# A Fourier filter ahead of a SiLU feed-forward block: sums and differences first, second products in eighths of the TensorE array, the complex filter on VectorE

## The chip, the cores and the metric

The kernel runs on one core of one Trainium2 chip. The metric is the time of one execution on the device in microseconds (us); lower is better. A figure from "the trace" comes from the hardware profiler's record of one execution. For the kernel before, the profiler took an execution of its own (3203.65 us). All runs told here are in the same, fast, state.

## The reference, cut to what matters

```python
# x: (8, 3008, 256)   filt_r, filt_i: (1505, 256)   w_in: (256, 2048)   w_out: (2048, 256)
X = np.fft.rfft(x, axis=1)
Y = X * (filt_r + 1j * filt_i)[None, :, :]
y = np.fft.irfft(Y, n=3008, axis=1)              # (8, 3008, 256), then (24064, 256)
h = y @ w_in
g = h * (1.0 / (1.0 + np.exp(-h)))               # SiLU
out = g @ w_out
```

The two dense products do most of the arithmetic. The transforms are done as matrix products too, by factors of 3008 = 47 x 64.

## The kernel before: the parts that matter

The names of the products are the names in the profile. For each of the 8 batches:

- **pa**: first products of the forward transform (47 points), already packed as four tiles of 47 rows by 64 columns.
- **pb**: second products (64 points), each a full 128 x 128 matrix. VectorE multiplies the result by the real and by the imaginary part of the filter (two tiles `p`).
- **pc**: first products of the inverse. The complex filter is completed here, by adding two products with two tables (`e_t[:, 0]` and `e_t[:, 1]`) in PSUM.
- **pd**: last products of the inverse; they give `y`.
- **ph** and **po**: the two dense products, with SiLU on ScalarE in between.

The dense work of a batch is 96 units; a unit is one ph piece and one po piece. The transforms of batch b+1 are cut into pieces that are placed by hand between the units of batch b. Batch 0 has nothing to hide behind: its transforms, the loading of all tables, and the rounding of the weights (VectorE turns 64-bit weights into 32-bit, 16 times) make the opening. In what follows, the opening ends at the first ph.

```python
def load_filters(g):                       # 4 calls, 16 loads of 192 KB, all issued by ScalarE's queue
    gs = slice(6 * g, 6 * g + 6)
    for k, filt in enumerate((filt_r, filt_i)):
        for q in range(2):
            off, step = (6 * g * C, C) if q == 0 else ((N1 - 6 * g) * C, -C)
            nc.scalar.dma_start(out=f_t[k][32 * q:32 * q + 32, gs, :],
                in_=bass.AP(tensor=filt.tensor, offset=filt.offset + off,
                            ap=[[N1 * C, 32], [step, 6], [1, C]]))   # 32 partitions x 6 rows

def evac(dst, src):                        # PSUM is emptied by VectorE and ScalarE in turn
    flip[0] ^= 1
    if flip[0]:
        nc.vector.tensor_copy(out=dst, in_=src)
    else:
        nc.scalar.copy(out=dst, in_=src)

def stage1(u):                             # pa, 8 pieces per batch
    ...
    for i in range(2):
        for h in range(2):
            rows = slice(64 * h, 64 * h + N1)
            nc.tensor.matmul(out=ps[h][64 * i:64 * i + 64], lhsT=wf_t[rows, :],
                             rhs=xt[rows, 2 * i:2 * i + 2, :], start=True, stop=True)
    for h in range(2):
        evac(t1[:, h], ps[h])
    ...                                    # t1 to DRAM, later read back as t2

def stage2(u):                             # pb and pc, 12 + 12 pieces per batch
    ...
        for i in range(2):
            nc.tensor.matmul(out=ps[:, i, :], lhsT=d_t[:, 2 * u + i, :], rhs=t2[:, i, :],
                             start=True, stop=True)
        ...
        for k in range(2):
            nc.vector.tensor_tensor(out=pt, in0=ps, in1=f_t[k][:, 2 * u:2 * u + 2, :], op=ALU.mult)
    ...
        for i in range(2):
            for k in range(2):
                nc.tensor.matmul(out=ps[:, i, :], lhsT=e_t[:, k, 2 * w + i, :],
                                 rhs=pr[k][:, i, :], start=(k == 0), stop=(k == 1))
    ...

at = UNITS * b                             # UNITS is 96
pieces  = [(at - 94 + 2 * u, lambda u=u: stage1(u)) for u in range(8)]
pieces += [(at - 75 + 2 * u, lambda u=u: stage2(u)) for u in range(13)]
pieces += [(at - 44 + 5 * u, lambda u=u: stage3(u)) for u in range(8)]         # pd, first half of y
pieces += [(at + 4 + 5 * u, lambda u=u: stage3(8 + u)) for u in range(8)]      # pd, second half
...
pending += [(-90 + 3 * j, NJ, lambda j=j: round_weights(j)) for j in range(NJ)]  # NJ is 16
```

## Time and profile before

| | before |
|---|---|
| time, median of 3 (range) | 3205.25 us (3203.8 to 3206.78) |
| ScalarE's first evacuation of PSUM | at 27.0 us |
| last evacuation of stage 1 of batch 0 | at 55.3 us |
| first ph (end of the opening) | at 155.6 us |
| one steady batch (first pa to first pa, mean of six) | 385.5 us |

Read it as a sum: 155.6 us of opening, then eight batches of dense work in which TensorE has hardly a hole (busy 383.29 of 385 us in a steady batch, 929 to 1314 us). A change is worth what it takes off the opening plus what it takes off each of the seven batches in which a following batch's transforms run. The busy table, the chain and the piece lines are shown and read in the prediction.

### The profile page before, as it was taken

What the parts mean: (1) busy time and instruction counts of PE and PEld (TensorE: products, weight loads), DVE (VectorE), ACT (ScalarE), POOL (GpSimd) and SP (SyncE); (2) the same over time, 40 slices, a digit from 0 to 9 for tenths busy, and PEclk for the clock granted to TensorE, in tenths of its full rate; (3) what the DMA queues carried; (4) which work ended last, traced back from release to release, by engine and by line L of the source; (5) the groups of instructions that cost most, each with busy time, mean ns of one, the idle gap of its engine ahead of it and who ended that gap; (6) DMA issues with size and microseconds to landing.
All of it is one profiled execution on the core that took longest, in us unless ns stands there. A gap on an engine that the chain in (4) does not pass through costs nothing.

```text
span 3201.7 us, 29583 instructions
## 1 busy us (share of the span) xinstructions
PE 3105.9 (97%) x11928; PEld 2096.2 (65%) x11928; DVE 353.7 (11%) x629; ACT 584.1 (18%) x1048; POOL 466.2 (15%) x884
## 2 busy tenths in 40 slices
PE   4699999999999999999999999999999999999999
PEld 2457666676666766667665676657766576666666
DVE  5701000110001100011000110011100110000000
ACT  1021111211111111211112111121111211111111
POOL 2121101211012101111102120031101211010101
PEclk9799999999999999999999999999999999999999
DMA  7532111221112211222102220032101221000000
GB/s 216 141 95 62 35 31 38 85 57 31 28 46 82 53 28 33 60 71 51 33 22 80 63 53 20 22 96 63 40 17 42 84 64 35 17 18 17 13 7 13
DMA packets 92583, 165.17 MB, mean 52 GB/s; under 512 B 24560, under 2 KB 56416, under 8 KB 92320
## 3 DMA queue, kind: packets, MB, share of 16 engines
q1 hardware_dynamic: 51456, 83.40, 9.3%
q0 software_dynamic: 38400, 75.04, 8.9%
q10 hardware_dynamic: 2592, 4.85, 0.6%
q8 instruction: 94, 1.54, 0.2%
q14 instruction: 41, 0.34, 0.0%
HBM read 88.21 MB, written 74.97 MB: 51 GB/s over the span
## 4 chain that ended last, share of the span: by engine, by line
PE 94%; DMA 1%; issue 1%; ACT 0%; DVE 0%; POOL 0%; POOLq 0%; DVEq 0%; ACTq 0%; SPq 0%
PE po L283 41%; PE ph L269 40%; PE pc L223 5%; PE pd L246 4%; PE pb L205 2%; PE pa L183 2%; DMA out_dram<-o 1%; ACT t L149 0%; DMA t<-d 0%; POOL out_dram L296 0%; ACT g L272 0%; DVE o L147 0%; DVE p L214 0%; DMA d<-q 0%; ACT o L149 0%
## 5 line engine op out<-in xcount | busy, mean ns | idle before, releaser
L283 PEld LDWEIGHTS po<-w,g 128*128 128x128 f32 (+1 forms) x6144 | 1152.4, 188 | 493.0 <-issue 353.8
L283 PE MATMUL po<-w,g 128*128 128x256 f32 (+1 forms) x6144 | 1455.0, 379 | 7.7 <-DVE o L147 5.4
L269 PE MATMUL ph<-y,w 128*128 128x512 f32 (+1 forms) x3072 | 1429.1, 588 | 0.0
L269 PEld LDWEIGHTS ph<-y,w 128*128 128x128 f32 x3072 | 572.4, 191 | 426.8 <-issue 389.4
L272 ACT ACTIVATE g<-ph 128x512 f32<-128x512 f32 (+1 forms) x768 | 452.0, 589 | 1961.1 <-PE ph L269 1960.9
L296 POOL DMA_DIRECT2D out_dram<-o x432 | 223.5, 525 | 1544.2 <-DVE o L147 1081.5
L229 POOL DMA_DIRECT2D d<-q x192 | 114.0, 598 | 803.1 <-DVE q L147 480.6
L223 PE MATMUL pc<-p,e_t 128*128 128x256 f32 x768 | 187.5, 388 | 9.5 <-DVE p L214 9.5
L214 DVE TENSOR_TENSOR p<-pb,filt 128x512 f32<-128x512 f32 x192 | 123.5, 686 | 614.2 <-PE pb L205 614.1
L190 POOL DMA_DIRECT2D d<-t x256 | 128.5, 509 | 384.2 <-DVE t L147 220.5
L147 DVE COPY o<-po 128x256 f32<-128x256 f32 x96 | 40.8, 425 | 1228.2 <-PE po L283 1181.3
L223 PEld LDWEIGHTS pc<-p,e_t 128*128 128x128 f32 x768 | 149.0, 195 | 32.9 <-DVE p L214 9.4
L246 PEld LDWEIGHTS pd<-wi_t,t 96*128 96x128 f32 x1024 | 138.0, 200 | 40.0 <-ACT t L149 22.9
L246 PE MATMUL pd<-wi_t,t 96*128 96x94 f32 x1024 | 139.3, 282 | 20.2 <-ACT t L149 10.5
L205 PE MATMUL pb<-t,d_t 128*128 128x256 f32 x384 | 102.6, 391 | 21.2 <-issue 10.3
L183 PE MATMUL pa<-x,wf_t 47*64 47x512 f32 x512 | 84.7, 673 | 29.4 <-DMA x<-in_x_dram 17.6
L205 PEld LDWEIGHTS pb<-t,d_t 128*128 128x128 f32 x384 | 74.1, 195 | 36.8 <-issue 12.4
L147 DVE COPY y<-pd 128x376 f32<-128x376 f32 x64 | 35.2, 550 | 556.7 <-PE pd L246 556.7
L147 DVE COPY t<-pa 128x512 f32<-128x512 f32 x64 | 44.2, 691 | 416.1 <-PE pa L183 413.7
L149 ACT COPY q<-pc 128x512 f32<-128x512 f32 x48 | 28.1, 586 | 220.1 <-PE pc L223 220.1
L149 ACT COPY t<-pa 128x512 f32<-128x512 f32 x64 | 37.5, 586 | 130.9 <-PE pa L183 121.7
L149 ACT COPY y<-pd 128x376 f32<-128x376 f32 x64 | 30.2, 472 | 164.6 <-PE pd L246 164.6
(24 smaller groups left out, 179.1 us busy)
## 6 DMA issues: line engine op xcount, KB each, us to landing
d<-t POOLq DMA_DIRECT2D x256, 96.0 KB, 2.8
t<-d SPq DMA_DIRECT2D x192, 128.0 KB, 2.7
d<-q POOLq DMA_DIRECT2D x192, 128.0 KB, 2.6
t<-d SPq DMA_DIRECT2D x64, 384.0 KB, 4.0
x<-in_x_dram SPq DMA_DIRECT2D x128, 128.0 KB, 2.8
x<-in_x_dram SPq DMA_DIRECT2D x128, 60.0 KB, 2.8
out_dram<-o POOLq DMA_DIRECT2D x80, 94.0 KB, 2.0
raw<-in_moe_w_in_dram SPq DMA_DIRECT2D x16, 256.0 KB, 3.2
```

The lines of the kernel that those rows point to most:

```text
L147: nc.vector.tensor_copy(out=dst, in_=src)
L183: nc.tensor.matmul(out=ps[h][64 * i:64 * i + 64], lhsT=wf_t[rows, :], rhs=xt[rows, 2 * i:2 * i + 2, :], start=True, stop=True)
L190: nc.gpsimd.dma_start(out=d1[:, n0:n0 + 2, :], in_=t1[64 * i:64 * i + 2 * NS, h])
L205: nc.tensor.matmul(out=ps[:, i, :], lhsT=d_t[:, 2 * u + i, :], rhs=t2[:, i, :], start=True, stop=True)
L214: nc.vector.tensor_tensor(out=pt, in0=ps, in1=f_t[k][:, 2 * u:2 * u + 2, :], op=ALU.mult)
L223: nc.tensor.matmul(out=ps[:, i, :], lhsT=e_t[:, k, 2 * w + i, :], rhs=pr[k][:, i, :], start=(k == 0), stop=(k == 1))
L229: nc.gpsimd.dma_start(out=d2[a0:a0 + 2, :, :].rearrange("s n c -> n s c"), in_=qt[64 * p:64 * p + 64, :, :])
L246: nc.tensor.matmul(out=psv[:, i, :], lhsT=t4s[g][:, i, cb * 128:cb * 128 + 128], rhs=wi_t, start=True, stop=True)
L269: nc.tensor.matmul(out=ps[:, 0:n], lhsT=w1[:, cb, 128 * j:128 * j + 128], rhs=cols[:, cb, c0:c0 + n], start=(cb == 0), stop=(cb == 1))
L272: nc.scalar.activation(out=g[:, 0:n], in_=ps[:, 0:n], func=AFT.Silu)
L283: nc.tensor.matmul(out=acc[t][0:m, 0:C], lhsT=g[:, 128 * t:128 * t + m], rhs=w2[:, j, :], start=(j == 0), stop=(j == NJ - 1))
L296: nc.gpsimd.dma_start(out=bass.AP(tensor=out.tensor, offset=out.offset + t0 * C, ap=[[32 * C, cnt], [1, C]]), in_=o[p:p + cnt, :])
```

## The change

The intent is to do less on TensorE. The input is first added to and subtracted from itself half a sequence away (`u`, on VectorE). This splits the frequencies into even and odd ones, and the second products shrink from 64 to 32 points: 64 rows by 32 columns each, so eight of them together have the size of one full 128 x 128 product. The complex filter is completed on VectorE (`z`), so that the inverse's first products need one table and not two, each of 64 rows by 128 columns, two of which have that size. The inverse's table is loaded instead of being made on the chip. The core of the diff, with the index tables cut:

```diff
+    d_t = cpool.tile([128, NS, 2, 32], FP32)          # was [128, NS, 128]
+    e_t = cpool.tile([128, NG, 2, 2, 128], FP32)      # was [128, 2, NS, 128], made on the chip
...
+    def load_filters():
+        for j in range(4):
+            ...
+            for half in range(2):
+                for k, filt in enumerate((filt_r, filt_i)):
+                    p0 = 32 * j + 16 * half
+                    nc.scalar.dma_start(
+                        out=f_t[k][p0:p0 + 16].rearrange("p g k c -> p (g k) c"),
+                        in_=bass.AP(tensor=filt.tensor, offset=filt.offset + off * C,
+                                    ap=[[94 * C, 16], [t * C, 2 * NG], [1, C]]))
...
+            if i == 0:
+                us[u] = upool.tile([128, 2, 4, C], FP32, ...)
+                for par, op in ((0, ALU.add), (1, ALU.subtract)):
+                    nc.vector.tensor_tensor(out=us[u][0:111, par], in0=xt[0:111, 0],
+                                            in1=xt[0:111, 1], op=op)
...
+        def forward(g):                                # pb
+            for ri in range(2):
+                for j in range(4):
+                    for k in range(2):
+                        rows = slice(64 * par, 64 * par + 64)
+                        nc.tensor.matmul(out=ps[k][32 * j:32 * j + 32, ri, :],
+                                         lhsT=d_t[rows, 4 * g + at, ri, :], rhs=t2[rows, at, :], ...)
+            for k in range(2):
+                for m in range(2):
+                    nc.vector.tensor_tensor(out=pt, in0=ps[k],
+                        in1=f_t[m][:, g, k:k + 1, :].to_broadcast([128, 2, C]), op=ALU.mult)
+                nc.vector.tensor_tensor(out=z[:, 0], in0=pr[0][:, 0], in1=pr[1][:, 1], op=ALU.subtract)
+                nc.vector.tensor_tensor(out=z[:, 1], in0=pr[0][:, 1], in1=pr[1][:, 0], op=ALU.add)
+        def inverse(g):                                # pc
+            for k in range(2):
+                for ri in range(2):
+                    for i in range(2):
+                        rows = slice(64 * i, 64 * i + 64)
+                        nc.tensor.matmul(out=ps[i][:, k, :], lhsT=e_t[rows, g, k, ri, :],
+                                         rhs=zs[k][rows, ri, :], start=(ri == 0), stop=(ri == 1))
...
-        pieces += [(at - 75 + 2 * u, lambda u=u: stage2(u)) for u in range(13)]
+        pieces += [(at - 75 + 4 * u, lambda u=u: forward(u)) for u in range(NG)]   # NG is 6
+        pieces += [(at - 73 + 4 * u, lambda u=u: inverse(u)) for u in range(NG)]
...
-    def inverse_tables():  ...                         # 24 transposes, 6 copies, 12 DVE operations
```

## The prediction

> **What bounds the kernel now.** I read the page's busy table and chain of waits first, then the table of engine busy time by stage, then the timeline around three transform pieces.
>
> ```profile
> PE 3105.9 (97%) x11928; PEld 2096.2 (65%) x11928; DVE 353.7 (11%) x629; ACT 584.1 (18%) x1048; POOL 466.2 (15%) x884
> ...
> PE po L283 41%; PE ph L269 40%; PE pc L223 5%; PE pd L246 4%; PE pb L205 2%; PE pa L183 2%; DMA out_dram<-o 1%; ACT t L149 0%; DMA t<-d 0%; POOL out_dram L296 0%; ACT g L272 0%; DVE o L147 0%; DVE p L214 0%; DMA d<-q 0%; ACT o L149 0%
> ```
>
> TensorE sets the end. 81% of the chain is the two dense products (ph, po), which the change leaves alone. All transforms together are about 13%: pc 5, pd 4, pb 2, pa 2. So even deleting pb and pc altogether could give only 7%.
>
> ```profile
> 0.00:156.00 156.00, 86.23 (x297) 54.30 (x298) 103.97 (x207) 14.49 (x26) 31.46 (x60) 0.84 0.66 180
> ...
> 929.00:1314.00 385.00, 383.29 (x1491) 259.54 (x1489) 34.63 (x58) 72.42 (x130) 58.15 (x110) 1.00 0.18 49
> ```
>
> Columns after the stretch and its length: PE, PEld, DVE, ACT, POOL busy, then granted clock, DMA share, GB/s. Two regimes. In the first 156 us there are only the transforms of batch 0 and the rounding of the weights: DVE is busy 104 us, PE 86. After that each batch takes 385 us with PE full; in its holes the next batch's transforms run, and DVE has only 35 us of work. What a PE piece costs is read from start to start, since the durations of pipelined matmuls overlap:
>
> ```profile
> 633.92 1.03 PE L205 MATMUL pb<-t,d_t 128*128 128x256 f32 x4
> 634.79 1.89 PE L223 MATMUL pc<-p,e_t 128*128 128x256 f32 x8
> 636.51 1.88 PE L269 MATMUL ph<-y,w 128*128 128x512 f32 x4
> ```
>
> One pb piece takes 634.79 - 633.92 = 0.87 us (4 instructions), one pc piece 1.72 us (8), so 0.215 us per instruction of 256 columns. (Each fp32 product stands as two instructions, in all counts below.) Both run back to back with the dense work at no cost of their own.
>
> ```profile
> 543.00 1.89 PE L283 MATMUL po<-w,g 128*128 128x256 f32 x8
> ...
> 544.55 0.42 DVE L147 COPY o<-po 128x256 f32<-128x256 f32 x1 [0.44 <-PE po L283]
> 544.82 0.21 PEld L183 LDWEIGHTS pa<-x,wf_t 47*64 47x64 f32 x8 [0.36 <-issue]
> 544.82 1.09 PE L183 MATMUL pa<-x,wf_t 47*64 47x512 f32 x8
> 545.84 0.30 PEld L269 LDWEIGHTS ph<-y,w 128*128 128x128 f32 x2 [0.81 <-issue]
> 545.84 1.98 PE L269 MATMUL ph<-y,w 128*128 128x512 f32 x4
> ...
> 547.66 1.89 PE L283 MATMUL po<-w,g 128*128 128x256 f32 x8
> ```
>
> pa is already packed in quarters of the array (47 rows by 64 columns). From 543.00 to 547.66 are 4.66 us; less 8 x 0.215 (po) and 4 x 0.43 (ph) leaves 1.22 us for pa. Eight 512-column instructions in sequence would be 3.43 us, in four tiles at once 0.86. So packing runs fully parallel here, and entering and leaving it costs 0.36 us: about 0.1 us before the first matmul, a weight load not hidden, and 0.1 us plus an unhidden 128-column load after it.
>
> [...] The trace has 686 ns for 512 elements [...] and 421 for 256 [...], so I take 1.22 us for the new ones of 1024.
>
> **The change part by part.** There are 7 batches in the steady part (batches 1 to 7; batch 0 is the opening), with 6 groups each.
>
> Second products, forward (pb). Now 24 full-array instruction pairs per batch: 48 x 0.215 = 10.3 us, 1.72 per group (two pb pieces). After: 32 instructions of 256 columns per group, in 64x32 tiles, 8 tiles at once, so 4 in sequence per tile = 0.86, skew of eight starts about 0.05, mode change about 0.33. Sum 1.24 us, saved 0.48 per group.
>
> First products of the inverse (pc). Now 2 x 1.72 = 3.44 us per group. After: 16 instructions per group, 64 rows by 128 columns, two at once: 8 x 0.215 = 1.72, plus mode change with a full-width load on both sides, 0.42. Sum 2.14, saved 1.30 per group.
>
> Together 1.78 per group: x 6 x 7 = 75 us off the PE chain.
>
> First products (pa): the same 32 products of 512 columns per batch in the same four quarters, so the PE time stays. Last products (pd): untouched.
>
> Vector engine, per batch: added 8 sums and differences x 1.22 = 9.8 us; the filter was 24 x 0.686 = 16.5 and becomes 24 x 0.686 + 24 x 0.421 = 26.6. So about 20 us more per batch on an engine with 35 of 385 busy: as throughput it is free. Its latency is not, because the schedule is in program order with two transform PSUM buffers. I went through the 96 units of a batch (a unit is one ph piece and one po piece, 3.44 us) and looked for pieces in which PE must now wait at once for DVE:
> - Start of a batch's stage 1 (unit 2): it follows the end of a chunk. DVE must first evacuate the chunk's outputs (the copy at 544.55, done at 544.97), then do the sum and the difference, 2 x about 1.2 us; in program order the sums stand behind these copies. The odd-half matmuls start near 547.4 and end near 548.3, where today pa ends near 545.7. Loss 2.6 us in six of the seven batches (at the first there is no chunk before): 15.6 us. The other sums have two or more units of lead.
> - Forward group 2 shares its unit with a pd piece. Both PSUM buffers are then with the new forward, and the first comes free after two filter products: 2 x 0.65 + about 0.15 = 1.45 us, x 7 = 10. Today a pc piece of 1.72 us lies between and hides it.
> - Inverse group 4 likewise, behind one evacuation of 0.69: 0.85 x 7 = 6.
> - The forward before a chunk end delays the output copies by some 4 us of DVE work: about 0.5 x 7 = 3.5.
> Sum of new waits: 35 us.
>
> DMA: the first intermediate goes in half as many stores of twice the size, loads likewise. The DMA share is 0.18 in the steady part; no effect.
>
> Opening (156 us). DVE works without a hole from 33 to 130 us. From the first weight rounding to the last filter operation: taken away are filter copies 8 x 0.95 = 7.6 and table work 12 x 0.43 = 5.2; added are sums 4 x 1.2 and the z operations 24 x about 0.37 (back to back), 8.9. That is nearly even. But two things worsen: the first forward can't start before the last stage 1 was stored and reloaded (stores 2 + 2.8, load about 3.3 us), time which the table work filled, and the inverse's last evacuation comes behind one more weight rounding (4.3 us), with three roundings left instead of two before DVE can copy the first y. Tables shrink by one (1.5 to 0.8 MB) and grow by one (1.5 MB), both in the background. I take +6 us (0 to 10).
>
> Sum: 3205 - 75 + 35 + 6 = 3171.
>
> **Rivals.**
> (a) The waits don't show and the opening is level: 3205 - 75 = 3130, 2.3% faster. For it: DVE is idle 90% of the steady part. Against: order, not load, makes these waits; today's trace already has PE waiting 0.7 us, 12 times, in the same pattern (pd behind stage 1, for an evacuation by ACT). Half of them hidden would make about 3150.
> (b) Eighths don't run eight at once: dispatch or reading eight moving streams limits them to four. Then a forward costs 4 x 2 x 0.215 + 0.4 = 2.1 us instead of 1.24: +36 us, 3207. For it: the trace before never shows more than four tiles or a matmul closer to the next in sustained terms than 0.107 us. Against: the pa loads and matmuls start some 7 ns apart, far from a limit.
> (c) DVE becomes the bound: 55 of 385 us per batch, no. Only in the opening, where it is counted; if DVE gaps there add up (each forward waits for an evacuation queued behind a rounding), +15 rather than +6, 3180.
> (d) The inverse's full-width weight loads in two row tiles serialise: 0.107 us each (pd's spacing is about 0.11), 16 of them = 1.7 us per group, just hidden under the 1.72. Little left even if so.
>
> **Range and chances.** 3171, with (a) and (b) on either side: 3143 to 3204 holds it 8 times in 10. Faster by over 2% needs under 3142, most of (a): 0.10. Slower by over 2% needs over 3269, for which packing would have to fail outright: 0.03. Within 2%: 0.87.
>
> **What would show it.** PE starts in the steady part: forward piece to the next ph 1.2 to 1.3 us, inverse piece 2.1 to 2.2. If the forward is near 2, (b). In the list of waits: PE pa for DVE u about six times at 2 to 2.6 us; PE pd for DVE p seven times near 1.4, and for DVE q near 0.8. First ph at about 162 us instead of 155.8. A steady batch of about 380 us instead of 385 (75 - 35 over 7 is 5.7). I am wrong if the batch is under 376 or over 386, or the first ph is before 154 or after 170.

The sum came to 3205 - 75 + 35 + 6 = 3171 us. This is what the prediction's figures stand on:

- Eight tiles at once for pb and two for pc (0.86 and 1.72 us) are my estimates. The trace before shows only four at once: pa's matmuls start in fours, 7 ns apart (544.819 to 544.839), and the next four follow 0.48 us after the first. The skew of eight is 7 x 7 ns.
- "Mode change" is the prediction's name for the cost of entering and leaving a packed piece, 0.36 us for pa. By the starts in that trace it consists of 0.09 us before pa's first matmul (544.51 + 0.215 to 544.82), 0.05 in its first four (0.48 against 0.43), 0.11 before the next ph (545.30 + 0.43 to 545.84) and 0.10 in the first matmul of that ph (0.53 against 0.43). That the 0.05 and the 0.10 are weight loads, of 64 and 128 columns, is my reading. The 0.33 us (32 columns at the start) and the 0.42 us (128) are estimates from these parts.
- The 1.22 us of a sum is the straight line through the trace's 421 ns for 256 elements and 686 ns for 512: 421 + 3 x 265 = 1216.
- The 0.107 us of rival (d) is an estimate too, from the 0.10 us above and from pd's matmuls, which start 0.11 us apart (688.92 to 689.67, eight of them).
- Of the new waits, the 0.15 us of handover is an estimate (in the trace before a filter product ends at 68.96 us and pc's weight load begins at 69.08), and so is the 0.5 us at the output copies.

## More of the kernel before

One line of the opening is needed later. It is from the groups of ScalarE's instructions by line, in the first 45 us: operation, count, busy us and mean ns, then how long the engine had been idle before and what it waited for.

```profile
L312 ACT ACT_TABLE_LOAD x1 | 1.3, 1283 | 25.6 <-DMA filt<-in_filt_r_dram 25.6
```

ScalarE does no work of its own before 25.6 us. Issuing loads does not count as work, and it issues sixteen filter loads one after the other. These issues are spread over the first 25 us (2.75 to 24.6), and the profile puts the wait down to the landing of filter loads. Every second evacuation of PSUM is ScalarE's, so stage 1 cannot get going until then: a pa piece waits 8.10 us for `ACT t`, up to 27.61 us.

## The result, and the profile after

Ratios here and below are the mean time of one kernel's fast runs over the mean of the other's fast runs of the same rounds, so they are not quite the ratio of the medians. The changed kernel took 3205.6 us (median of 4, 3197.63 to 3206.49) beside 3206.02 for the kernel before; ratio 0.9994, 95% interval 0.9977 to 1.0012. The class predicted as likeliest (within 2%) came, but the time is outside the range, and the expected 1% is not there.

| | before | after | predicted |
|---|---|---|---|
| ScalarE's first evacuation | 27.0 | 39.7 | |
| last evacuation of stage 1, batch 0 | 55.3 | 78.7 | |
| first ph | 155.6 | 184.2 | about 162 |
| first ph to the end of the span | 3046.1 | 3011.7 | 40 less |
| steady batch | 385.5 | 381.1 | about 380 |

The steady part gained 34.4 us and the opening lost 28.6. In the traces that makes 3201.7 - 34.4 + 28.6 = 3195.9, which is the span of the profiled execution (3197.63 us as timed). The other three executions of that round were 7 to 9 us longer. I have no trace of those.

The steady part first. The page of the changed kernel has these lines for busy time and for the chain by product:

```profile
PE 3034.0 (95%) x13056; PEld 1969.8 (62%) x13056; DVE 481.7 (15%) x865; ACT 581.4 (18%) x1042; POOL 405.1 (13%) x758
...
PE 90%; DVE 4%; DMA 4%; issue 1%; ACT 1%; POOL 1%; SPq 0%; DVEq 0%; ACTq 0%; POOLq 0%
PE ph L333 40%; PE po L347 40%; PE pd L309 4%; PE pc L285 3%; PE pa L233 2%; PE pb L259 2%; DMA out_dram<-o 2%; DVE p L269 1%; DMA x<-in_x_dram 1%; POOL out_dram L360 0%; DVE u L225 0%; DVE z L275 0%; DMA filt<-in_filt_r_dram 0%; DMA raw<-in_moe_w_in_dram 0%; DMA t<-d 0%
```

TensorE is busy 72 us less, and pc has gone from 5% of the chain to 3%. But TensorE's share of the chain has also gone from 94% to 90%: VectorE and DMA now carry 4% each, where the kernel before had 0% and 1%. The work was saved, and something else has come onto the path.

The saving, piece by piece, in TensorE's timeline after (start, length, line, operation, tiles, shapes, count):

```profile
650.88 1.89 PE L347 MATMUL po<-w,g 128*128 128x256 f32 x8
652.70 1.09 PE L259 MATMUL pb<-t,d_t 64*32 64x256 f32 x32
653.72 1.98 PE L333 MATMUL ph<-y,w 128*128 128x512 f32 x4
655.54 1.89 PE L347 MATMUL po<-w,g 128*128 128x256 f32 x8
...
658.99 1.89 PE L347 MATMUL po<-w,g 128*128 128x256 f32 x8
660.81 2.00 PE L285 MATMUL pc<-z,e_t 64*128 64x256 f32 x16
662.73 1.98 PE L333 MATMUL ph<-y,w 128*128 128x512 f32 x4
664.55 1.67 PE L347 MATMUL po<-w,g 128*128 128x256 f32 x7
```

From 650.88 to 655.54 are 4.66 us; less a po piece (1.72) and a ph piece (1.72) leaves 1.22 us for 32 matmuls in eighths. From 658.99 to 664.55 are 5.56, which leaves 2.12 for the inverse piece. Predicted were 1.24 and 2.14.

The new waits are as foreseen too. What TensorE waited for in the steady part, after (from 186 to 3196 us) and before (160 to 3202): total us, times, longest.

```profile
PE pd L309 <- ACT t L195: 10.7, 14, 0.8
PE pd L309 <- DVE p L269: 10.7, 7, 1.5
PE po L347 <- DVE o L193: 9.9, 8, 1.6
PE pa L233 <- DVE u L225: 8.6, 7, 1.4
PE pd L309 <- ACT q L195: 4.7, 7, 0.7
PE po L347 <- ACT o L195: 4.1, 9, 0.6
```

```profile
PE pd L246 <- ACT t L149: 10.5, 14, 0.8
PE po L283 <- DVE o L147: 5.4, 6, 2.6
PE po L283 <- ACT o L149: 2.2, 1, 2.2
```

The sums are 48.7 and 18.1 us, so 30.6 more. The wait for `ACT t` was there before the change.

At the batch boundary the trace shows the sums behind the output copies, and a pa piece cut in two:

```profile
568.62 0.42 DVE L193 COPY o<-po 128x256 f32<-128x256 f32 x1 [0.44 <-PE po L347]
568.97 2.35 DVE L225 TENSOR_TENSOR u<-x 111x1024 f32<-111x1024 f32 x2
...
570.33 2.12 PE L233 MATMUL pa<-u,wf_t 47*64 47x512 f32 x8 [1.36 <-DVE u L225]
```

TensorE waits 1.36 us for the sum. The piece then takes 2.05 us to the next ph instead of 1.02, since its second half waits for the difference; the list of waits does not show that second part. It happens in all seven batches (in the first of them after a wait of only 0.38 us), so it is 7 x 1.03 = 7.2 us. Altogether 30.6 + 7.2 = 37.8 us of new waits.

Now the opening. First ScalarE's line in the first 45 us, after:

```profile
L377 ACT ACT_TABLE_LOAD x1 | 1.3, 1283 | 38.3 <-DMA filt<-in_filt_r_dram 38.3
```

ScalarE is free at 38.3 us instead of 25.6. The issues of the filter loads, with KB each and median us from issue to landing, before and then after:

```profile
filt<-in_filt_r_dram ACTq DMA_DIRECT2D x8, 192.0 KB, 5.9
filt<-in_filt_i_dram ACTq DMA_DIRECT2D x8, 192.0 KB, 5.9
```

```profile
filt<-in_filt_r_dram ACTq DMA_DIRECT2D x8, 192.0 KB, 9.4
filt<-in_filt_i_dram ACTq DMA_DIRECT2D x8, 192.0 KB, 9.9
```

The same bytes take 1.6 times as long. And what TensorE did meanwhile. First, from the kernel before, the piece with its longest wait in this stretch and the first pb; then the stage after:

```profile
27.61 1.98 PE L183 MATMUL pa<-x,wf_t 47*64 47x512 f32 x6 [8.10 <-ACT t L149]
...
64.24 2.05 PE L205 MATMUL pb<-t,d_t 128*128 128x256 f32 x4 [6.84 <-DMA t<-d]
```

```profile
21.36 1.96 PE L233 MATMUL pa<-u,wf_t 47*64 47x512 f32 x2 [0.78 <-DVE t L193]
40.29 1.98 PE L233 MATMUL pa<-u,wf_t 47*64 47x512 f32 x6 [16.97 <-ACT t L195]
44.27 3.02 PE L233 MATMUL pa<-u,wf_t 47*64 47x512 f32 x8 [2.01 <-DVE u L225]
48.00 2.04 PE L233 MATMUL pa<-u,wf_t 47*64 47x512 f32 x8 [0.71 <-ACT t L195]
58.50 3.02 PE L233 MATMUL pa<-u,wf_t 47*64 47x512 f32 x8 [8.46 <-DVE u L225]
62.27 2.05 PE L233 MATMUL pa<-u,wf_t 47*64 47x512 f32 x8 [0.76 <-ACT t L195]
70.64 2.16 PE L233 MATMUL pa<-u,wf_t 47*64 47x512 f32 x6 [6.32 <-DVE u L225]
```

Two effects stand one after the other: 16.97 us of waiting for ScalarE, and then 2.01, 8.46 and 6.32 us of waiting for the sums, with the weight roundings on VectorE in between (two of them from 47.93 to 57.1 us, one from 64.97 to 69.3). Where the trace before has its first pb at 64.24 us, stage 1 is not over here.

VectorE's own account, from its first continuous work to the first ph (stretch, its length, then PE, PEld, DVE, ACT, POOL busy, clock, DMA share, GB/s), before and then after:

```profile
32.70:155.60 122.90, 75.89 (x273) 52.36 (x273) 102.53 (x204) 11.77 (x21) 27.10 (x48) 0.80 0.59 169
```

```profile
42.30:184.20 141.90, 71.77 (x401) 40.10 (x401) 107.06 (x215) 9.04 (x16) 22.73 (x40) 0.76 0.54 150
```

The loss of 28.6 us is 9.6 (it starts later) + 4.5 (its work: 107.06 - 102.53) + 14.5 (idle: 34.84 - 20.37). The work is nearly even, as the prediction had it. The lateness was not in the prediction. Most of the added idle time lies after stage 1, where VectorE waits for the forward pieces. The waits of VectorE in these stretches, before and then after (total us, times, longest):

```profile
DVE p L214 <- PE pb L205: 1.6, 1, 1.6
```

```profile
DVE p L269 <- PE pb L259: 12.8, 4, 8.2
```

The longest, 8.2 us, is for the first pb, which itself waits for the store and the load of the last stage 1 (11.61 us for `DMA t<-d`, to 88.07 us; stores and loads of this size take 4.1 us each to land, as a median). Before, the table work stood in that place (56.05 to 61.4 us). The prediction had named that wait.

The same account for stage 1 alone, from VectorE's first evacuation after ScalarE is free to the last of the stage, before and then after:

```profile
29.63:55.34 25.71, 18.04 (x59) 5.47 (x60) 20.19 (x43) 4.95 (x9) 12.51 (x24) 1.00 0.90 268
```

```profile
42.30:78.66 36.36, 15.19 (x48) 2.94 (x48) 27.18 (x49) 4.11 (x7) 6.45 (x12) 1.00 0.55 169
```

Both hold seven evacuations and four roundings. Stage 1 starts 12.7 us later here and takes 10.7 us longer: 7.0 us of work, which is three pairs of sums, and 3.7 us of idle time. From its end to the first ph 5.2 us more are lost (105.5 against 100.3). So of the 28.6 us, 23.4 are lost by the end of stage 1.

### The profile page after: what moved, and what is told of

It reads as the page before. It is cut to its first block, busy times and chain, and to the rows that moved or that the text cites. A ratio compares the mean times of both kernels' runs of the same rounds, so it can differ in the third digit from the quotient of the medians.

```text
span 3195.9 us, 31337 instructions
## 1 busy us (share of the span) xinstructions
PE 3034.0 (95%) x13056; PEld 1969.8 (62%) x13056; DVE 481.7 (15%) x865; ACT 581.4 (18%) x1042; POOL 405.1 (13%) x758
## 4 chain that ended last, share of the span: by engine, by line
PE 90%; DVE 4%; DMA 4%; issue 1%; ACT 1%; POOL 1%; SPq 0%; DVEq 0%; ACTq 0%; POOLq 0%
PE ph L333 40%; PE po L347 40%; PE pd L309 4%; PE pc L285 3%; PE pa L233 2%; PE pb L259 2%; DMA out_dram<-o 2%; DVE p L269 1%; DMA x<-in_x_dram 1%; POOL out_dram L360 0%; DVE u L225 0%; DVE z L275 0%; DMA filt<-in_filt_r_dram 0%; DMA raw<-in_moe_w_in_dram 0%; DMA t<-d 0%
## 5 line engine op out<-in xcount | busy, mean ns | idle before, releaser
L309 PE MATMUL pd<-wi_t,t 96*128 96x94 f32 x1024 | 140.7, 284 | 38.7 <-DMA t<-d 12.1
L309 PEld LDWEIGHTS pd<-wi_t,t 96*128 96x128 f32 x1024 | 137.9, 200 | 63.1 <-issue 26.8
L233 PE MATMUL pa<-u,wf_t 47*64 47x512 f32 x512 | 90.7, 674 | 62.8 <-DVE u L225 42.8
L285 PE MATMUL pc<-z,e_t 64*128 64x256 f32 x768 | 113.3, 422 | 20.1 <-DVE z L274 16.1
L241 POOL DMA_DIRECT2D d<-t x128 | 65.8, 521 | 486.8 <-DVE t L193 250.6
L285 PEld LDWEIGHTS pc<-z,e_t 64*128 64x128 f32 x768 | 80.4, 203 | 50.2 <-issue 42.3
L233 PEld LDWEIGHTS pa<-u,wf_t 47*64 47x64 f32 x512 | 17.2, 140 | 104.6 <-issue 48.6
L225 DVE TENSOR_TENSOR u<-x 111x1024 f32<-111x1024 f32 x64 | 75.3, 1218 | 20.8 <-DMA x<-in_x_dram 20.8
L259 PE MATMUL pb<-t,d_t 64*32 64x256 f32 x1536 | 58.8, 392 | 18.4 <-DMA t<-d 12.4
L193 DVE COPY q<-pc 128x512 f32<-128x512 f32 x48 | 33.1, 691 | 224.4 <-PE pc L285 137.7
```

The source lines that it names most:

```text
L225: nc.vector.tensor_tensor(out=us[u][0:111, par], in0=xt[0:111, 0], in1=xt[0:111, 1], op=op)
L233: nc.tensor.matmul(out=ps[h][64 * par:64 * par + 64], lhsT=wf_t[rows, par], rhs=ut[rows, par, 2 * i:2 * i + 2, :], start=True, stop=True)
L259: nc.tensor.matmul(out=ps[k][32 * j:32 * j + 32, ri, :], lhsT=d_t[rows, 4 * g + at, ri, :], rhs=t2[rows, at, :], start=True, stop=True)
L285: nc.tensor.matmul(out=ps[i][:, k, :], lhsT=e_t[rows, g, k, ri, :], rhs=zs[k][rows, ri, :], start=(ri == 0), stop=(ri == 1))
L309: nc.tensor.matmul(out=psv[:, i, :], lhsT=t4s[g][:, i, cb * 128:cb * 128 + 128], rhs=wi_t, start=True, stop=True)
```

## The experiments

Two theories were put to the test. **A**: the loss in the opening comes from the filter loads, whose new shape holds ScalarE (and so the first evacuations) up. **B**: it comes from the sums, which stand between the x loads and the first products and queue behind the weight roundings. **A'** is a form of A in which the issuing engine is to blame and not the traffic. For the steady part, the theory is that the saving is whole and the waits listed above eat half of it; the rival is that the packed pieces cost more elsewhere. Landmarks are in us from each run's trace; times are medians of four. The traced execution need not be the median one: openafter's took 3170.36 us, 8 us less than its median.

| run | ScalarE's first evacuation | last of stage 1 | first ph | batch | time | ratio to before (95%) |
|---|---|---|---|---|---|---|
| again | 39.7 | 78.7 | 183.6 | 381.05 | 3198.86 | 0.9982 (0.9967 to 0.9997) |
| nosum | 32.0 | 65.3 | 169.1 | 378.7 | 3167.44 | 0.9881 (0.9862 to 0.9899) |
| poolq | 13.8 | 71.3 | 177.8 | 380.2 | 3192.46 | 0.9959 (0.9944 to 0.9974) |
| fshape | 34.1 | 73.1 | 178.8 | 381.5 | 3193.85 | 0.9968 (0.9948 to 0.9987) |
| steady | 41.2 | 78.0 | 184.6 | 373.7 | 3147.67 | 0.9833 (0.9818 to 0.9847) |
| bshape | 34.2 | 67.6 | 168.1 | 385.1 | 3215.64 | 1.0042 (1.0027 to 1.0057) |
| openafter | 12.3 | 38.7 | 154.8 | 381.1 | 3178.53 | 0.9923 (0.9907 to 0.9939) |
| openbefore | 7.1 | 34.0 | 142.8 | 385.65 | 3189.43 | 0.9961 (0.9945 to 0.9978) |
| both | 28.8 | 59.7 | 164.4 | 379.0 | 3162.55 | 0.9871 (0.9854 to 0.9887) |
| beforeunits | 26.8 | 55.2 | 157.1 | 383.45 | 3192.28 | 0.9969 (0.9954 to 0.9984) |
| roundlate | 37.2 | 63.4 | 181.1 | 381.65 | 3194.43 | 0.9979 (0.9964 to 0.9994) |
| best | 12.3 | 39.1 | 155.7 | 373.15 | 3117.46 | 0.9736 (0.9722 to 0.9751) |

The kernel before ran beside them at medians of 3204.51 (first four), 3201.65 (next four) and 3201.68 us (last four).

**again: the changed kernel, unedited**, as the base for the others.

> The changed kernel once more, as a control. Its four times were 3197.6 to 3206.5 us and the profiled run was the fastest, so its opening (first ph at 184.2 us against 155.6 before) may be the short case. If the spread comes from the opening, a run of 3205 us shows a first ph near 192 us and the same steady batches of 381 us; if from the steady part, first ph stays at 184 us and the batches are over 382.

3198.86 us (3195.18 to 3202.4), ratio 0.9982. The landmarks are those of the first trace within 0.6 us. So the opening's loss is the same each time. Both traces are of executions at the short end of their rounds, so they do not say why the median of the first round was 7 us longer; that stays open.

**nosum: no sums and differences.** The first products read x itself. The result is wrong.

```diff
-                us[u] = upool.tile([128, 2, 4, C], FP32, ...)
-                xt = x_t[u % 2]
-                for par, op in ((0, ALU.add), (1, ALU.subtract)):
-                    nc.vector.tensor_tensor(out=us[u][0:111, par], in0=xt[0:111, 0],
-                                            in1=xt[0:111, 1], op=op)
+                us[u] = x_t[u % 2]
```

> Wrong on purpose: the sums and differences are left out and the first products read x itself. Chain theory (the opening lost time to several waits in series, the sums behind weight roundings being about 10 us of the 28): first ph 10 to 12 us earlier, near 173 us, and the six waits of pa for u in the steady part (about 2.5 us each with the split pa) gone, batches from 381 to about 379; in all 24 to 27 us faster, near 3180 us. Traffic theory (the opening is late because of loads): first ph within 3 us of 184, total only some 15 us faster.

The first ph comes 14.5 us earlier than in "again", and stage 1 ends 13.4 us earlier. Only 4 x 2 x 1.22 = 9.8 us of operations went, of which the prediction had booked half. So leaving the sums out takes back about half of the loss. But that half is not all time of the sums: ScalarE's first evacuation also comes 7.7 us earlier (32.0 against 39.7), stage 1 is only 5.7 us shorter, and the rest loses 1.1 us less. The issues of the first twelve x loads show what else the edit changed, in the changed kernel and then here (start, length):

```profile
1.77 20.54 SPq L210 DMA_DIRECT2D x<-in_x_dram  x12
```

```profile
1.77 34.62 SPq L209 DMA_DIRECT2D x<-in_x_dram  x12
```

The sums copy x out of its buffers, so that the third group of x can be loaded at once; without them the last of these loads, and the weight loads after them, come 14 us later and no longer run beside the filter loads. That fits ScalarE's earlier release; no run tests it by itself. So the run mixes A and B: the sums cost their own time, and they also bring traffic forward. The total is lower than expected (3167) because each batch also became 2.35 us shorter, which is the boundary wait.

**poolq: GpSimd's queue issues the tables and filters**, same loads, same order.

```diff
-                    nc.scalar.dma_start(            # the filters; the same edit for d_t, e_t, wi_t
+                    nc.gpsimd.dma_start(
```

> The loads of the tables and filters are issued by GpSimd, which is idle then, and no longer by ScalarE, whose first evacuation came at 39.7 us behind these issues (27.0 before). Chain theory: first evacuation by ScalarE before 22 us, first ph some 13 us earlier, near 171 us, total near 3192 us. If VectorE's amount of work sets the opening, or the amount of traffic, first ph stays within 4 us of 184.

ScalarE now evacuates at 13.8 us, 26 us sooner, and the first ph gains 6 us. The rest came back as another wait. The waits between 20 and 60 us have this line:

```profile
DVE e L401 <- DMA raw<-in_moe_w_out_dram: 17.0, 1, 17.0
```

VectorE stands at the second weight rounding, to 45.4 us, for its raw weights. The filter loads are in flight in the same time: a filter load takes 14.4 to 14.8 us to land here (9.9 to 10.4 in "again"), GpSimd waits for landings of filters up to 45.4 us, and from 30 to 40 us the DMA share is 1.04, at 153 GB/s. So another issuer did not make the loads faster in this run: 26 us of ScalarE's time became 6 us of the kernel's. A' falls as the main cause.

**fshape: the changed kernel with the filter loads in the old shape**, 32 partitions x 6 rows. The filters land in the wrong places, so the result is wrong; bytes, issues and loads are unchanged.

```diff
-                        out=f_t[k][p0:p0 + 16].rearrange("p g k c -> p (g k) c"),
-                                    ap=[[94 * C, 16], [t * C, 2 * NG], [1, C]]))
+                        out=f_t[k][32 * g:32 * g + 32].rearrange("p g k c -> p (g k) c")[:, 6 * q:6 * q + 6],
+                                    ap=[[N1 * C, 32], [step, 6], [1, C]]))
```

> Wrong on purpose: the filters are loaded in the shape of the kernel before (32 partitions by 6 rows for each load) in place of 16 partitions by 12 rows, the same bytes and number of loads. If the shape is what made a filter load land in 9.4 us instead of 5.9 and held ScalarE 12.7 us longer, the first evacuation by ScalarE returns to about 27 us and the total falls by about 12 us, to 3193. If it is the x loads beside them (now twice as large, running two groups ahead) ScalarE stays held to 36 us or more and the total stays at 3205.

ScalarE comes 5.6 us sooner and the first ph 4.8 us sooner. The median landing went from 9.4 to 8.0 us, not to the 5.9 of the kernel before. So the shape counts, but by less than ScalarE's 12.7 us of lateness had led me to think.

**bshape: the kernel before with the new shape**, 16 partitions x 12 rows. Its output is wrong, which doesn't matter for the time. This is the converse of fshape.

```diff
-                    out=f_t[k][32 * q:32 * q + 32, gs, :],
-                                ap=[[N1 * C, 32], [step, 6], [1, C]]))
+                    out=f_t[k][16 * g:16 * g + 16, 12 * q:12 * q + 12, :],
+                                ap=[[94 * C, 16], [t, 12], [1, C]]))
```

> Wrong on purpose: the kernel before, its filters loaded in the changed kernel's shape (16 partitions by 12 rows), everything else as it was. The mirror of the run that gave the changed kernel the old shape and brought ScalarE's first evacuation from 39.7 to 34.1 us. If the shape costs about 5 us by itself, the first evacuation goes from 27.0 to about 32 us and the first ph from 155.6 to about 160; if it costs only beside the larger x loads, both stay within 2 us.

The shape alone, in a kernel with no sums in it, delays ScalarE's first evacuation by 7.2 us and the first ph by 12.5, and costs 0.4% of the time. The landing time and the rates show where. First the issue line of this run, then the stretch from 20 to 40 us in the kernel before, in bshape and in the changed kernel (last two columns: DMA share, GB/s).

```profile
filt<-in_filt_r_dram ACTq DMA_DIRECT2D x8, 192.0 KB, 9.3
```

```profile
20.00:40.00 20.00, 8.62 (x30) 1.92 (x30) 7.67 (x16) 3.72 (x6) 7.03 (x14) 1.00 1.03 257
```

```profile
20.00:40.00 20.00, 4.11 (x15) 0.70 (x14) 0.69 (x1) 2.54 (x4) 3.48 (x7) 1.00 1.08 130
```

```profile
20.00:40.00 20.00, 2.55 (x4) 0.28 (x2) 0.69 (x1) 1.72 (x3) 0.00 (x0) 1.00 1.07 179
```

The DMA engines are equally full by their records (share 1.03 to 1.08), yet they move 257 GB/s before and 130 in bshape. So a full DMA share was not a full rate here. (The three stretches do not hold the same transfers: before, the last filter load is issued at about 24 us.) The landing times go the same way in both kernels: 5.9 us for 32 partitions before and 9.3 to 9.5 for 16 in bshape, 8.0 in fshape and 9.4 to 9.9 in the changed kernel. The row runs changed along with the partitions (6 rows, then 12), so these runs show the cost of the shape, and not which part of it makes it.

**both: fshape and nosum together**. Its output is wrong, which doesn't matter for the time.

> Wrong on purpose: the changed kernel without the sums and with the filters loaded in the old shape. Alone, leaving out the sums brought the first ph from 183.9 to 169.1 us, and the old shape brought it to 178.8; the kernel before with the new shape went from 155.6 to 168.1. If these two are the whole of the loss of the opening, the first ph comes to 153 to 160 us. If a third thing (the longer work of the complex filter, or the order of roundings and evacuations at the end of stage 2) counts beside them, it stays above 163.

The first ph is at 164.4 us. That is 19 us better than "again", about the sum of the two parts (14.5 + 4.8), and 8.8 us worse than the kernel before. Half of the 8.8 is there at the end of stage 1 (59.7 against 55.3), and half comes after it. The half after it is near what the prediction had worked out for the rest of the opening. So the loss splits into about 14.5 for what goes with the sums (7.7 of it by way of ScalarE), 5 for the shape, and 9 for all else. What the first half of that last part is (x loads twice as large, which land in 5.8 us instead of 2.8; the e_t load of 1536 KB, which lands in 12.0) I did not separate.

**roundlate: the weight roundings start after stage 1.** If VectorE's queue ahead of the sums is what costs, they should come sooner.

```diff
-        pending += [(-90 + 3 * j, NJ, lambda j=j: round_weights(j)) for j in range(NJ)]
+        pending += [(-79 + (34 * j) // 15, NJ, lambda j=j: round_weights(j)) for j in range(NJ)]
```

> Correct. The changed kernel with the weight roundings of the opening put after stage 1 instead of between its pieces; same work, other order. If the sums cost the opening because they stand behind roundings, the last evacuation of stage 1 comes at about 66 us in place of 78.7 and the first ph at about 176 in place of 184. If the opening is bound by VectorE's amount of work alone, the first ph stays within 3 us of 184.

Stage 1 ends 15.3 us earlier, and the first ph only 2.5 us earlier. The roundings still have to be done before the first dense product, so VectorE pays for its idle time at the front with the roundings at the back (it is busy 4.3 us of the first 41, and 106.1 of the 140 up to 181). So the roundings ahead of the sums make stage 1 late, as B has it, but they do not make the first ph late: it came at 181 us and not at the 176 named for that case. It stayed within the 3 us named for a bound by VectorE's amount of work, and ScalarE alone was 2.5 us earlier here (37.2 against 39.7).

**openafter: the opening of the changed kernel reordered.** All of batch 0's x is loaded first, then the tables and filters, and seven roundings are put off into the dense part (weights of later blocks are not needed at once).

```diff
-    nc.scalar.dma_start(out=d_t, in_=d_dram.ap())       # also e_t, wi_t and the filters
+    pending = [(-85, 50, tables)]                        # the same loads, on nc.sync, after the x loads
-        pending.append((-95, NJ, lambda: load_weights(0)))
-        pending += [(-90 + 3 * j, NJ, lambda j=j: round_weights(j)) for j in range(NJ)]
+        pending.append((-85, 51, lambda: load_weights(0)))
+        pending += [(-74 + 3 * j if j < 9 else 2 * j - 17, 99, lambda j=j: round_weights(j))
+                    for j in range(NJ)]
```

> Correct. The changed kernel with its opening rearranged: x of batch 0 is loaded first, the tables and filters after it on the same queue, the weights last; no rounding stands between the pieces of stage 1, and the last 7 of the 16 roundings are moved into the first units of the dense work. Traffic and order theory (the full DMA queues of the first 45 us, then 16 roundings between the steps, set the opening): first ph near 138 us, 45 us earlier than in the changed kernel, total near 3155 us. If the sums and the complex filter on VectorE by themselves made the opening long, first ph stays above 165 us.

The first ph came at 154.8 us where I had expected 138. Stage 1 ends at 38.7, and then the waits of TensorE up to 155 us have this line:

```profile
PE pb L259 <- DMA t<-d: 21.8, 2, 21.7
```

The load of the first intermediate now stands behind the tables that had been put off: it is issued at 53.11 us, after the issues of the tables and filters on the same queue (22.1 to 45.2 us). It is the same exchange as in poolq: what is in flight is moved, not less.

**openbefore: the same reordering for the kernel before** (tables and the first weights at unit -82).

> Correct. The kernel before with the same rearrangement of its opening. If the changed kernel's loss lay in the opening only, then with both openings relieved the change should be worth what the steady part gives, about 30 us less the remaining difference of the openings: this run near 3180 us with the first ph near 132 us, and 20 to 30 us slower than the changed kernel so rearranged.

The first ph is at 142.8 us. With both openings reordered alike, the changed kernel is 12.0 us behind in the first ph and 4.55 us per batch ahead. The two totals, 3178.53 and 3189.43, differ by 10.9 us, where I had expected 20 to 30.

**steady: only the steady part's order changed.** The sums become a piece of their own, a unit ahead of their products, and the pieces of the last stage move to units where no other piece takes both PSUM buffers.

```diff
-        pieces = [(at - 94 + 2 * u, lambda u=u: stage1(u // 2, u % 2)) for u in range(8)]
+        pieces = [(at - 97 if u == 0 else at - 95 + 4 * u, lambda u=u: sums(u)) for u in range(4)]
+        pieces += [(at - 94 + 2 * u, lambda u=u: stage1(u // 2, u % 2)) for u in range(8)]
-        pieces += [(at + 4 + 5 * u, lambda u=u: stage3(8 + u)) for u in range(8)]
+        pieces += [(at + (3, 9, 15, 20, 24, 28, 32, 36)[u], lambda u=u: stage3(8 + u)) for u in range(8)]
```

> Correct. The changed kernel with the sums of a group issued as a piece of their own, ahead of their matmuls and ahead of the chunk's output copies, and with the second half of the last products moved to units that hold no forward or inverse piece. If the new waits of the steady part are what the prediction said (pa for u six times, pd behind forward, pd behind inverse, 30 to 35 us in all, measured by the trace of the changed kernel at about 31 with the split pa), the batches fall from 381 to near 377 us and the total by 25 to 30 us, to about 3170. If those waits only take the place of others, the total stays within 8 us of the changed kernel's.

3147.67 us: about 51 us better than "again" (on another chip), and 1.7% better than the kernel before. The gain is larger than expected. In part that is because the edit also took away the wait for `ACT t` (10.7 us), which the kernel before has too. The waits of TensorE that are left from 192 us on:

```profile
PE po L350 <- DVE o L193: 12.0, 8, 1.9
PE po L350 <- ACT o L195: 1.7, 3, 0.7
```

The batch went from 381.05 to 373.7 us; times seven that is 51. The listed waits, with the split pa, fell by some 41 us; the other 10 have no line. Nothing of the arithmetic was changed, so the order of the pieces is what kept most of the saving from showing. The next run shows how little is left for the rival (packed pieces that cost more elsewhere).

**beforeunits: the kernel before with the same units for the last stage**, to see how much of that gain is not the change's.

```diff
-        pieces += [(at + 4 + 5 * u, lambda u=u: stage3(8 + u)) for u in range(8)]
+        pieces += [(at + (3, 9, 15, 20, 24, 28, 32, 36)[u], lambda u=u: stage3(8 + u)) for u in range(8)]
```

> Correct. The kernel before with the second half of the last products moved to the same units as in the run that removed the waits from the changed kernel (3147.7 us). It separates what of those 50 us belongs to waits which the change brought from waits that were there before: the trace of before has pd waiting 14 times for 0.75 us behind stage 1. Expected 8 to 11 us faster than before, near 3193; if 20 or more, much of that run's gain isn't the change's.

The batch falls by 2.05 us, to 383.45. So old waits were worth 2 us per batch. With these gone on both sides the change is worth 383.45 - 373.7 = 9.75 us per batch (predicted from the pieces: 75 / 7 = 10.7; so at most about 1 us per batch is left for the rival), and the waits that it brought are 381.1 - 373.7 - 2.05 = 5.3 us per batch (predicted: 35 / 7 = 5.0).

**best: openafter and steady together.**

> Correct. Both corrections together: the opening rearranged (3178.5 us alone) and the sums and last products moved (3147.7 us alone). If they act on different stretches, the gains add: first ph near 155 us, batches near 373.7, total near 3125 us.

3117.46 us (3115.67 to 3118.67), ratio 0.9736, correct: 2.6% faster than the kernel before. The opening and a steady batch, in the columns used above:

```profile
0.00:155.70 155.70, 76.53 (x417) 40.98 (x417) 81.94 (x156) 11.10 (x19) 26.26 (x46) 0.82 0.66 164
929.00:1314.00 385.00, 383.68 (x1684) 250.57 (x1683) 55.17 (x93) 75.02 (x135) 52.16 (x98) 1.00 0.21 52
```

The first ph is back where the kernel before had it (155.7 against 155.6), with nine roundings and not sixteen ahead of it, so VectorE has 82 us of work there. In the steady stretch TensorE is busy 383.68 of 385 us again, and it gets more done in it. Not all of the 2.6% is the change's. The reordered opening alone brought the kernel before to a ratio of 0.9961 (openbefore), the new units of the last stage alone to 0.9969 (beforeunits). If these add, which was not run, the change itself is worth about 2.0% (0.9736 / (0.9961 x 0.9969) = 0.980).

## Why the prediction was wrong, point by point

**What bounds the kernel, and the two regimes: right.** The opening and the batches moved apart from one another, and their sum is the result.

**75 us off TensorE: right.** The pieces cost 1.22 and 2.12 us (predicted 1.24 and 2.14). Eight tiles of a forward piece do run at once: in the trace after, eight matmuls of pb start between 652.70 and 652.75 us, and the next eights 0.24, 0.46 and 0.67 us after them. Both of its row tiles write both PSUM tiles (`ps[k]` gets the row tile `par` equal to `k` for even `j` and the other for odd `j`). Beyond its own streaming a packed piece between full-array pieces cost 0.36 us (forward: 1.22 less 4 x 0.215) and 0.40 us (inverse: 2.12 less 8 x 0.215). Rival (b), only four tiles at once, would have needed 2.1 us for the forward piece and falls. Rival (d), serial weight loads hidden under the products (by its estimate 1.7 us under 1.72), would cost next to nothing, so the 2.12 us do not test it.

**35 us of new waits: right in sum, 37.8.** In its terms: the batch boundary 8.6 + 7.2 = 15.8 us (predicted 15.6); pd behind a forward 10.7 (10); pd behind an inverse 4.7 (6); output copies 9.9 + 4.1 against 5.4 + 2.2 before, so 6.4 more (3.5). The middle one, as the trace has it:

```profile
687.83 1.09 PE L259 MATMUL pb<-t,d_t 64*32 64x256 f32 x32
690.45 1.10 PE L309 MATMUL pd<-wi_t,t 96*128 96x94 f32 x8 [1.53 <-DVE p L269]
```

Rival (a), that these waits stay hidden, falls with it. The steady part gained 34.4 us instead of 40; 75 - 37.8 would be 37.2, and the 3 us between I could not place.

**The opening, +6 us: this is the step that failed.** It measured +28.6 (+28.0 in "again"). The account ran "from the first weight rounding to the last filter operation" and took everything before as level. But 23.4 of the 28.6 us are lost by the end of stage 1. Two of its steps were wrong:

- The tables were said to load "in the background". No load that ScalarE issues in the first 38 us is in the background here: ScalarE is free only when all are issued (38.27 us), and every second evacuation of stage 1 waits for ScalarE (TensorE's 16.97 us of waiting for `ACT t`). That start came 12.7 us later. The diff shows the new shape of the filter loads, and I did not look at it because its bytes are the same. The old shape put back brought ScalarE 5.6 us forward (fshape), the sums left out 7.7 (nosum), and both together 10.9, to 28.8 us. Put into the kernel before, the new shape alone cost 12.5 us of first ph (bshape).
- VectorE's work was called "nearly even". That is correct as a sum (4.5 us more, of 102.5), but a sum is not what counts. The operations that were taken away (table work, filter copies) lay after stage 1; the sums that came stand in it. The prediction booked two pairs (4 x 1.2 us; the trace after has a median of 1217 ns for one). Three pairs stand between ScalarE's start and the end of stage 1, for 7.0 us, with 3.7 us more of waiting around them.

Rival (c), gaps of VectorE that add up behind the forwards, had +15. These gaps came (12.8 us of waits for pb against 1.6), but they are not where the time went: from the end of stage 1 to the first ph only 105.5 - 100.3 = 5.2 us were lost, which is what the +6 had really worked out. That VectorE works "without a hole from 33 to 130 us" was not exact either: the trace before has holes of 2.3, 2.3 and 1.6 us there.

With the two measured terms, 3205 - 75 + 37.8 + 28.6 = 3196, about what the profiled execution took (3197.63) and the median of "again" (3198.86). The 3205.6 of the first round is 7 us more than that; the landmarks of the two traces are the same, so the opening does not explain it, and it is left open.

## What to carry to other kernels

In an opening that nothing hides, cost a change by its place in the chain and not by the balance of an engine's busy time: ask for every added operation what it waits for and who waits for it. Look at the shape of each load (the partitions that it lands in, and the length of its rows), even where the bytes stay: in bshape 16 partitions x 12 rows in place of 32 x 6 landed in 9.3 us and not 5.9, and the first ph came 12.5 us later. Look also at which engine stands in the queue to issue it. And when a saving on the bounding engine shows up as new short waits, move the pieces in the schedule before giving the change up: here the same arithmetic was worth 0.2% as written and 2.6% with the order mended, of which about 2.0% would be the change's own.
